# Attention and expert router on one core: sums of weights behind the centroids' products, codes behind the result's copy, first additions on GpSimd, logits and a drain earlier

## The chip, the cores and the metric

The kernel runs on one core of a Trainium2 chip. The core has TensorE (PE, matmuls; its weight loads are shown apart as PEld), VectorE (DVE), ScalarE (ACT), GpSimd (POOL) and SyncE (SP, which here issues most DMAs). Each engine works through its own queue in order. The metric is device time in microseconds (us) for one execution, less is better.

## The reference

The first half is attention inside clusters. Every query and every key of a head goes to the one of 16 centroids that it is nearest to, and a query attends only to keys of its own cluster. The second half sends every token (a row of all heads' results) to the one of 8 experts that it is nearest to, and multiplies that expert's result by the softmax weight of the choice.

```python
B, H, S, D = 4, 8, 768, 64          # 16 centroids per head
q_assign = argmax(q_n @ c_n.T); k_assign = argmax(k_n @ c_n.T)   # rows of unit length
scores = where(q_assign == k_assign, q @ k.T / sqrt(D), -1e9)
x = softmax(scores) @ v              # (B, H, S, D), then to (3072, 512)
logits = unit(x) @ unit(expert_emb).T / tau                      # 8 experts
e = argmax(logits); gate = softmax(logits)[e]
out = gate * (relu(x @ w1[e]) @ w2[e])       # w1 512x1024, w2 1024x512
```

All of it is in float32, apart from the cluster masks, which are exact in bfloat16.

## The kernel before

**Attention.** Two heads of one batch make a pair; there are 16 pairs, numbered n = 0 to 15, four for each batch b. A pair's work is cut into 12 units: two halves of the queries (groups 2n and 2n+1), and for each six blocks of 128 keys (j = 0 to 5). The main loop takes two units an iteration, so a pair has six iterations, it = 0 to 5. In an iteration the order is written out by hand: the scores of the next two units go to PE (`scores`, L484) and their exponentials to ACT (`expo`, L495); then `between(n, it)` puts in pieces of the next pair's preparation and of routing; then the two units of this iteration are multiplied with the values (`attend`, L506).

The exponentials are written to five rotating buffers, `probs`. A buffer is free for the exponential five units later when PE has read it in `attend` and when it has been added to `acc`, the running sum of the group's weights. The sum of the first two units (j = 1) is one instruction on DVE, L515, which also adds a tiny constant; the four that follow are plain additions, L525. Only two score buffers exist (`psS`), so the scores of a unit wait for the exponential of the unit two before.

**Behind a group.** After j = 5 ACT copies the group's result out of PSUM (`o_sb`, L530) and `unite` adds its two halves on GpSimd (L539; on DVE for the last pair). `total` sums `acc` over partitions on PE with a matrix of ones (L553) in a `misc` bank, of which there are two in turn; DVE transposes and inverts, and GpSimd spreads the inverses with eight small copies (L574). `divide` multiplies the result with the inverses (L585, L589), and `rows` transposes it and stores it to `x_rows` in HBM (L606, L613). `total` for a pair's two groups is called in the next pair's iteration 0 behind `attend`; `divide` in its iteration 2, `rows` in its iteration 3.

**Preparing a pair.** `prep_pieces` gives the steps: `turn0` and `turn1` transpose the queries and keys on DVE (L386), `products` multiplies them with the centroids on PE (L396) and transposes the outcome back on DVE (L405), `choose` finds the nearest centroid on DVE (L414 to L417), writes its code with three activations on ACT (`cd`, L419 and L422) and has SP transpose the codes by DMA into `hot` (L427). The scores of the next pair, which begin in iteration 5, read `hot`: a matmul of the codes adds the mask (L484, the bfloat16 ones).

```python
elif it == 0:
    piece(n + 1, "products")
elif it == 1:
    piece(n + 1, "choose")
elif it == 3:
    rows(2 * n - 2, 2 * n - 1)
```

The matmuls of scores and results use the array in four parts of 64x64; those of `products`, `total` and the router's logits use four parts of 128x32.

**Routing and experts.** A batch's router products (L632) and logits (`lt`, L644) are made in the next batch's pairs. For the last batch they come after the loop, in two halves: `route[b][0](0)`, the products of the first half, closes the loop; `logits(0)` and `products(1)` come later, among the first experts' blocks. From there PE works through the experts' blocks to the end: `hidden` L1261, `result` L1277, and for larger portions L1176 and L1213. GpSimd gathers tokens (L1041) and scatters results (L1052) with indirect DMAs. In the last attention pairs GpSimd also gathers the first experts' tokens (`fetch`, three in pair 14, iteration 3) and orders them (`order_x`, L1127).

Of the kernel before, what the change touches and what calls it, by code (L numbers as in the profile page):

```python
# [39 lines left out]
def kernel(  # L40
# [282 lines left out]
    def begin():  # L323

        nc.scalar.dma_start(out=c_sb, in_=centroids.rearrange("h c d -> (h c) d"))
        load(0, "q")
        load(0, "k")
        load(0, "v")
        load(1, "qk")
        constants()  # L330

        nc.scalar.activation(en_r, epsc[0:E], ACTF.Sqrt)
        nc.scalar.dma_start(out=emb, in_=moe_expert_emb)
        nc.scalar.dma_start(out=tau, in_=moe_tau.to_broadcast([E, 1]))
        norm_rows(cn_r, c_sb, P)
        unit_centroids()
        keep_up(2)
        piece(0, "turn0")
        piece(0, "turn1")
        norm_rows(en_r, emb, E)  # L340

        nc.scalar.activation(cn_r, epsc, ACTF.Exp)
        piece(0, "products")
        for m in range(2):
            scores(m, (1,))
        piece(0, "choose")
        keep_up(6)
        piece(0, "turn_numbers")
        for m in range(2):
            scores(m, (0,))  # L350
            expo(m)
        token_numbers()
        unit_experts()

    def prep_pieces(n):
# [51 lines left out]
        def choose():  # L407

            shp = [P, S // SQ, C]
            asn = t["asn"].rearrange("p (g c) -> p g c", c=C)  # L410
            amax = smp.tile(shp[0:2], F32, tag="amax", name="amax")
            sel = smp.tile(shp, BF16, tag="sel", name="sel", bufs=1)
            pm = smp.tile(shp[0:2], BF16, tag="pm", name="pm")
            nc.vector.tensor_reduce(amax, asn, axis=AXX, op=ALU.max)  # L414
            nc.vector.tensor_tensor(sel, asn, bc(amax, shp, 2), ALU.is_equal)
            nc.vector.tensor_tensor(sel, sel, bc(prefc, shp, 1), ALU.mult)
            nc.vector.tensor_reduce(pm, sel, axis=AXX, op=ALU.max)  # L417
            pm = pm.rearrange("p (s h) -> p s h", h=2)
            nc.scalar.activation(cd[..., 1], pm, ACTF.Copy, scale=wcd)  # L419
            for i, p0 in enumerate((0, D)):  # L420
                g = slice(p0, p0 + D)
                nc.scalar.activation(  # L422
                    cd[g, :, :, 2 * i], pm[g], ACTF.Square, scale=(BIG**0.5, 1.0)[i]
                )
            t["H"] = trp.tile([P, S // (2 * SQ), P], BF16, tag="hot", name="hot")
            if n > 0:
                nc.sync.dma_start_transpose(  # L427
                    out=t["H"], in_=cd.rearrange("p s h c -> p (s h c)")
                )

        def turn_numbers():
# [17 lines left out]
            "turn1": lambda: turn_blocks("k") if n else (turn("q", 1), turn("k", 1)),  # L449
            "products": products,  # L450
            "choose": choose,
            "turn_numbers": turn_numbers,
        }

# [42 lines left out]
    def attend(i):  # L497

        n, hq, j = units[i]
        d, g = un[i], gr[i // GU]  # L500
        if j == 0:
            g["o_ps"] = psO.tile([P, 2, 512], F32, tag="o_ps", name="o_ps")
        for h in range(2):
            for half in range(2):
                keys = slice(D * half, D * half + D)
                nc.tensor.matmul(  # L506
                    g["o_ps"][D * h : D * h + D, half, 0:HE],
                    lhsT=ld[n]["v"][keys, j, h],
                    rhs=d["prob"][keys, h, 0:HE],
                    start=(j == 0),  # L510
                    stop=(j == NJ - 1),
                )
        if j == 1:
            g["acc"] = xp.tile([P, 2, HS], F32, tag="acc", name="acc", bufs=3)
            nc.vector.scalar_tensor_tensor(  # L515
                out=g["acc"],
                in0=un[i - 1]["prob"][:, :, 0:HS],
                scalar=NJ * EPS,
                in1=d["prob"][:, :, 0:HS],
                op0=ALU.add,  # L520
                op1=ALU.add,
            )
            un[i - 1].clear()
        elif j > 1:
            nc.vector.tensor_tensor(g["acc"], g["acc"], d["prob"][:, :, 0:HS], ALU.add)  # L525
            d.clear()
        if j == NJ - 1:
            t = ld[n]
            t["o_sb"] = xp.tile([P, 2, HE], F32, tag="o_sb", name="o_sb", bufs=1)
            nc.scalar.copy(t["o_sb"], g["o_ps"][:, :, 0:HE])  # L530
# [801 lines left out]
    def between(n, it):  # L1332
        b, nb = divmod(n, NHP)
        if n == 0:

            if it == 0:
                piece(1, "turn0")
                piece(1, "turn1")
            elif it == 1:
                piece(1, "products")  # L1340
            elif it == 2:
                piece(1, "choose")
                turned_experts()
            elif it == 3:
                later_constants()
        elif it == 0:
            piece(n + 1, "products")
        elif it == 1:
            piece(n + 1, "choose")
        elif it == 3:  # L1350
            rows(2 * n - 2, 2 * n - 1)
        if it == 4:
            piece(n + 2, "turn0")
        elif it == 5:
            piece(n + 2, "turn1")
        if b > 0:
            if nb == 0 and it == 3:
                route[b - 1] = route_pieces(b - 1)
            products, logits, read, norms, choose = route.get(b - 1, (None,) * 5)


            m = NJ * nb + it
            if m in (8, 11, 14):
                read((m - 8) // 3 * 2, (m - 8) // 3 * 2 + 2)
            if m in (15, 16, 18, 19, 21, 22):
                norms((15, 16, 18, 19, 21, 22).index(m))
            if (nb, it) == (0, 4):
                products(0, 1)
            elif (nb, it) == (0, 5):
                logits(0, 1)  # L1370
            elif (nb, it) == (1, 4):
                choose()
# [29 lines left out]
    with tc.manual_schedule(engines=by_hand):  # L1402
        begin()
        for i in range(0, len(units), 2):
# [21 lines left out]
                turn_x(E0[0], nc.scalar.copy, xp.tile([P, DM], F32, tag="acc", name="xTm", bufs=3))  # L1426
            for m in range(i, i + 2):
                attend(m)
            if it == 2:
                if n > 0:  # L1430
                    divide(2 * n - 2, 2 * n - 1)
                unite(2 * n)
            elif it == 5:
                unite(2 * n + 1)
            if i + 2 == len(units):
                rows(ngroups - 2)
                route[b][0](0)
            if it == 0 and n > 0:
                total(2 * n - 2, 2 * n - 1)
            elif it == 3 and n == NP - 1:  # L1440
                total(2 * n)
        at.close()
        mop = ctx.enter_context(tc.tile_pool(name="mop", bufs=2, **tile_waits))
# [9 lines left out]
        pb = Places(1, rtb)  # L1453
        gates = gate_pieces(0, B - 1)
        gates[0]()
        hidden(E0[0], (0,))
        order_x(E0[3])
        total(ngroups - 1)
# [7 lines left out]
        hidden(E0[0], (1,))  # L1466
        gates[3]()
        weights1(E0[2])
        logits(0)
        read(0, NJ, P - SQ, P)  # L1470
        products(1)
        hidden(E0[1], (0,))
# [83 lines left out]
        for i, it in enumerate(later):  # L1556
# [9 lines left out]
                fetch(later[i + 2])  # L1566
            if i > 0 and later[i - 1].kind == "sized":
                send(later[i - 1])
            if it.kind == "sized":
                sized_hidden(it)  # L1570
            else:
# [66 lines left out]
```

## Time and profile before

| what | us |
|---|---|
| median of 3 timed runs | 716.82 (714.88 to 720.92) |
| the profiled execution's own time | 709.36 |
| its span, first to last instruction | 707.6 |
| PE busy in the span | 690.8 (98%) |
| attention loop, about | 16 to 334 |
| experts, about | 334 to 701 |

The profiled execution was faster than each of the three timed ones; times of steps come from it. "PE busy" contains modelled ends of matmuls, so it is read beside the times at which PE's matmuls start. A line of the timeline has its start in the span, its duration, the engine, the source line, what was done and how many instructions were merged; in square brackets stands how long the engine had been idle, and what ended that.

### The profile page before, as it was taken

How to read it: one execution, taken by the hardware profiler on the slowest of the kernel's cores; microseconds unless marked ns; L12 is line 12 of the kernel's file. 1: busy time of each engine (PE TensorE's matmuls, PEld its weight loads, DVE VectorE, ACT ScalarE, POOL GpSimd, SP SyncE). 2: the span in 40 equal slices, each digit the busy share in tenths (PEclk: the TensorE clock that was granted, in tenths of full speed). 3: DMA queues.
4: the chain of work that ended last, by engine and by line, in shares of the span. 5: the costliest groups of instructions: out<-in, count | busy, mean ns of one | idle time of the engine just before them, and what ended most of it. 6: DMA issues, size and time to landing. Idle time of an engine off the chain costs nothing.

```text
span 707.6 us, 16122 instructions
## 1 busy us (share of the span) xinstructions
PE 690.8 (98%) x6518; PEld 456.2 (64%) x6518; DVE 382.6 (54%) x665; ACT 265.1 (37%) x446; POOL 264.2 (37%) x402
## 2 busy tenths in 40 slices
PE   6999999999999999999899999999999999999995
PEld 3444444444444444455876668897979797979793
DVE  4788888989889999989483121340220303031210
ACT  4566665677566755676215110101010111111110
POOL 2122222322224222353213546736264554544412
PEclk9999999999999999999999999999999999999999
DMA  9536665886657678879798987268668686869450
GB/s 150 91 60 110 105 104 87 153 159 108 100 108 146 120 146 152 183 190 329 184 278 305 342 314 268 81 233 287 258 226 299 198 310 226 320 242 330 142 192 28
DMA packets 244124, 135.55 MB, mean 192 GB/s; under 512 B 207808, under 2 KB 207810, under 8 KB 244044
## 3 DMA queue, kind: packets, MB, share of 16 engines
q1 hardware_dynamic: 237852, 121.28, 64.0%
q0 software_dynamic: 6016, 13.12, 5.4%
q8 instruction: 54, 0.88, 0.5%
q14 instruction: 26, 0.21, 0.1%
q10 hardware_dynamic: 176, 0.05, 0.0%
HBM read 115.92 MB, written 13.12 MB: 182 GB/s over the span
## 4 chain that ended last, share of the span: by engine, by line
PE 79%; DVE 6%; DMA 5%; issue 5%; POOL 1%; SPq 1%; ACT 1%; POOLq 0%; DVEq 0%; ACTq 0%
PE s_ps L484 18%; PE o_ps L506 15%; PE y_ps L1277 10%; PE h_ps L1261 9%; PE h_ps L1176 9%; PE y_ps L1213 5%; PE misc L1213 5%; DMA out_dram<-ys,spidx 3%; PE x_ps L1176 3%; DVE acc L525 2%; DMA x_rows<-xb 2%; PE misc L396 2%; PE misc L553 2%; PE misc L632 1%; SPq L613 1%
## 5 line engine op out<-in xcount | busy, mean ns | idle before, releaser
L495 ACT ACTIVATE prob<-s_ps 128x768 f32<-128x768 f32 x192 | 153.7, 812 | 95.2 <-PE s_ps L484 82.1
L484 PE MATMUL s_ps<-qT,kT 64*64 64x384 f32 x1536 | 156.0, 482 | 0.0
L506 PE MATMUL o_ps<-prob,v 64*64 64x385 f32 x1536 | 142.0, 486 | 0.0
L525 DVE TENSOR_TENSOR acc<-acc,prob 128x768 f32<-128x768 f32 x128 | 125.6, 982 | 8.8 <-ACT cd L422 0.5
L506 PEld LDWEIGHTS o_ps<-prob,v 64*64 64x64 f32 x1536 | 54.6, 133 | 70.3 <-issue 58.5
L1261 PE MATMUL h_ps<-xTm,w1s 128*128 128x128 f32 x768 | 90.0, 278 | 0.0
L1261 PEld LDWEIGHTS h_ps<-xTm,w1s 128*128 128x128 f32 x768 | 89.0, 195 | 1.4 <-issue 1.0
L1222 DVE STREAM_TRANSPOSE ys<-y_ps 128x256 f32<-128x256 f32 (+4 forms) x16 | 6.7, 417 | 153.4 <-PE y_ps L1213 153.4
L539 POOL TENSOR_TENSOR o_sum<-o_sb 128x385 f32<-128x385 f32 x30 | 32.0, 1067 | 146.3 <-ACT o_sb L530 146.3
L1052 POOL DMA_INDIRECT out_dram<-ys,spidx x56 | 56.7, 1013 | 74.7 <-DVE ys L1236 59.8
L1277 PE MATMUL y_ps<-w2s,hT 128*128 128x512 f32 x192 | 84.5, 593 | 0.0
L484 PEld LDWEIGHTS s_ps<-qT,kT 64*64 64x64 f32 x1536 | 56.0, 133 | 38.1 <-issue 34.9
L1176 PE MATMUL h_ps<-xTs,w1s 128*128 128x272 f32 (+7 forms) x384 | 72.9, 346 | 1.1 <-ACTq L1537 1.1
L1176 PEld LDWEIGHTS h_ps<-xTs,w1s 128*128 128x128 f32 x384 | 66.6, 190 | 8.0 <-issue 2.4
L1268 ACT ACTIVATE hT<-h_ps 128x512 f32<-128x512 f32 x24 | 14.3, 596 | 148.1 <-PE h_ps L1261 148.1
L484 PE MATMUL s_ps<-hot 64*64 64x384 bf16 x768 | 64.7, 325 | 2.2 <-ACT prob L495 1.1
L1041 POOL DMA_INDIRECT xs<-x_rows,gpidx x56 | 57.3, 1023 | 17.1 <-issue 16.8
L574 POOL COPY inv<-inv 32x12 f32<-32x12 f32 x120 | 43.0, 358 | 54.6 <-DVE inv L571 50.2
L1277 PEld LDWEIGHTS y_ps<-w2s,hT 128*128 128x128 f32 x192 | 35.6, 190 | 40.2 <-issue 40.2
L484 PEld LDWEIGHTS <-hot 64*64 64x64 bf16 x768 | 23.6, 106 | 39.4 <-issue 38.1
L1213 PE MATMUL y_ps<-hTs,w2o 128*128 128x272 f32 (+7 forms) x256 | 48.0, 346 | 0.0
L1213 PE MATMUL misc<-hTs,w2o 128*128 128x272 f32 (+7 forms) x256 | 48.0, 346 | 0.0
(264 smaller groups left out, 679.5 us busy)
## 6 DMA issues: line engine op xcount, KB each, us to landing
w1s<-in_moe_w_dram SPq DMA_DIRECT2D x18, 2048.0 KB, 10.6
w2s<-in_moe_w_dram SPq DMA_DIRECT2D x18, 2048.0 KB, 13.3
v<-in_v_dram SPq DMA_DIRECT2D x128, 48.0 KB, 2.1
q<-in_q_dram SPq DMA_DIRECT2D x60, 96.0 KB, 3.4
k<-in_k_dram SPq DMA_DIRECT2D x60, 96.0 KB, 3.6
x_rows<-xb SPq DMA_DIRECT2D x60, 96.0 KB, 2.8
xr<-x_rows SPq DMA_DIRECT2D x9, 512.0 KB, 4.0
w1s<-in_moe_w_dram SPq DMA_DIRECT2D x4, 1024.0 KB, 9.9
```

Source lines behind the costliest of these rows:

```text
L484: nc.tensor.matmul(s_ps[D * half : D * half + D, h, 0:HS], lhsT=l[rows, half], rhs=r[rows], start=part == (1 if len(parts) < 2 else 0), st ...
L495: nc.scalar.activation(d["prob"][:, :, 0:HS], d["s_ps"][:, :, 0:HS], ACTF.Exp, scale=scale)
L506: nc.tensor.matmul(g["o_ps"][D * h : D * h + D, half, 0:HE], lhsT=ld[n]["v"][keys, j, h], rhs=d["prob"][keys, h, 0:HE], start=(j == 0), st ...
L525: nc.vector.tensor_tensor(g["acc"], g["acc"], d["prob"][:, :, 0:HS], ALU.add)
L539: add(t["o_sum"][:, hq], t["o_sb"][:, 0], t["o_sb"][:, 1], ALU.add)
L574: nc.gpsimd.tensor_copy(inv2[M * to : M * to + M, :, i % 2], inv[M * i : M * i + M])
L1041: nc.gpsimd.indirect_dma_start(out=to, out_offset=None, in_=of, in_offset=bass.IndirectOffsetOnAxis(ap=at, axis=0), bounds_check=n - 1, oo ...
L1052: inst = nc.gpsimd.indirect_dma_start(out=to, out_offset=bass.IndirectOffsetOnAxis(ap=at, axis=0), in_=of, in_offset=None, bounds_check=n - 1,
L1176: nc.tensor.matmul(bk, lhsT=w1s[it.slot][:, c, P * f : P * f + P], rhs=d["xT"][:, c, 0:C], start=(c == 0), stop=(c == KD - 1),)
L1213: nc.tensor.matmul(bks[g][:, 0:C], lhsT=d["w2"][:, f, P * g : P * g + P], rhs=d["hT"][:, f, 0:C], start=(f == 0), stop=(f == KF - 1),)
L1261: nc.tensor.matmul(bk[:, m : m + P], lhsT=w1s[it.slot][:, c, f0 + m : f0 + m + P], rhs=d["xT"][:, P * c : P * c + P], start=(c == 0), stop ...
L1277: nc.tensor.matmul(bk, lhsT=d["hT"][:, P * c : P * c + P], rhs=w2s[it.slot][:, c], start=(c == 0), stop=(c == KF - 1),)
```

## The change

- `choose` is cut in two: the activations on ACT and the DMA of the codes become a piece of their own, `codes`, called in iteration 2 after `attend`, behind the result's copy of that iteration.
- In a pair's loop `turn0` of pair n+2 moves from iteration 4 to 5, `turn1` of the next pair from iteration 5 to the following iteration 0, `products` from 0 to 1, `choose` from 1 to 2, `rows` from 3 to 4. `total` moves from iteration 0 behind `attend` to iteration 1, directly behind `products`. `divide` moves from 2 to 3, `unite` of the first group from 2 to 3 and of the second from iteration 5 to the next pair's iteration 0. The earlier batches' router products move from iteration 4 to 5, their logits from 5 to the next pair's iteration 0.
- The first addition of each group (j = 1) goes to GpSimd as a plain addition, and the tiny constant is added at j = 2 on DVE, in the form that L515 had.
- For the last batch `logits(0)` moves ahead of the first expert's `hidden`.
- GpSimd gets a `drain` behind the last large scatter, ahead of the last block's scatter.

```diff
         piece(0, "choose")
+        piece(0, "codes")
...
-            pm = pm.rearrange("p (s h) -> p s h", h=2)
+            t["pm"] = pm.rearrange("p (s h) -> p s h", h=2)
+
+        def codes():
+            pm = t["pm"]
             nc.scalar.activation(cd[..., 1], pm, ACTF.Copy, scale=wcd)
...
         if j == 1:
             g["acc"] = xp.tile([P, 2, HS], F32, tag="acc", name="acc", bufs=3)
+            nc.gpsimd.tensor_tensor(
+                g["acc"], un[i - 1]["prob"][:, :, 0:HS], d["prob"][:, :, 0:HS], ALU.add
+            )
+            un[i - 1].clear()
+        elif j == 2:
             nc.vector.scalar_tensor_tensor(
                 out=g["acc"],
-                in0=un[i - 1]["prob"][:, :, 0:HS],
+                in0=g["acc"],
                 scalar=NJ * EPS,
                 in1=d["prob"][:, :, 0:HS],
                 op0=ALU.add,
                 op1=ALU.add,
             )
-            un[i - 1].clear()
+            d.clear()
...
         elif it == 0:
+            piece(n + 1, "turn1")
+        elif it == 1:
             piece(n + 1, "products")
-        elif it == 1:
+            total(2 * n - 2, 2 * n - 1)
+        elif it == 2:
             piece(n + 1, "choose")
-        elif it == 3:
+        elif it == 4:
             rows(2 * n - 2, 2 * n - 1)
-        if it == 4:
+        if it == 5:
             piece(n + 2, "turn0")
-        elif it == 5:
-            piece(n + 2, "turn1")
...
-            if (nb, it) == (0, 4):
+            if (nb, it) == (0, 5):
                 products(0, 1)
-            elif (nb, it) == (0, 5):
+            elif (nb, it) == (1, 0):
                 logits(0, 1)
...
+            if it == 0 and n > 0:
+                unite(2 * n - 1)
             if it == 2:
-                if n > 0:
-                    divide(2 * n - 2, 2 * n - 1)
+                piece(n + 1, "codes")
+            if it == 3 and n > 0:
+                divide(2 * n - 2, 2 * n - 1)
+            if it == (3 if n + 1 < NP else 2):
                 unite(2 * n)
-            elif it == 5:
+            elif it == 5 and n + 1 == NP:
                 unite(2 * n + 1)
...
-            if it == 0 and n > 0:
-                total(2 * n - 2, 2 * n - 1)
-            elif it == 3 and n == NP - 1:
+            if it == 3 and n == NP - 1:
                 total(2 * n)
...
         gates[0]()
+        logits(0)
         hidden(E0[0], (0,))
...
-        logits(0)
         read(0, NJ, P - SQ, P)
         products(1)
...
                 send(later[i - 1])
+                if i == LAST:
+                    nc.gpsimd.drain()
```

More of the change, by code (lines that the diff above doesn't have):

```diff
@@ L451, in prep_pieces @@
             "choose": choose,
+            "codes": codes,
             "turn_numbers": turn_numbers,
```

## The prediction

> **What bounds the kernel now.** I read the page's busy times first, then the same by stages, then PE's waits, then the timeline of one pair.
>
> ```profile
> PE 690.8 (98%) x6518; PEld 456.2 (64%) x6518; DVE 382.6 (54%) x665; ACT 265.1 (37%) x446; POOL 264.2 (37%) x402
> ...
> 193.96:213.29 19.33, 19.33 (x268) 8.80 (x264) 15.96 (x26) 11.86 (x17) 6.12 (x12) 1.00 0.56 112
> ...
> 253.27:275.22 21.95, 21.75 (x301) 10.05 (x297) 21.08 (x31) 12.53 (x18) 6.02 (x11) 1.00 0.80 149
> ...
> PE s_ps L484 <- ACT prob L495: 1.1, 2, 0.7
> ...
> PE misc L632 <- DVE lt L644: 2.1, 1, 2.1
> ```
>
> PE is never idle for long. The rows by stage are pair 9 and pair 12 (length; then busy time of PE, PEld, DVE, ACT, POOL; clock; DMA share and GB/s): in pair 9 DVE works 15.96 of 19.33 us, in pair 12 21.08 of 21.95, so there DVE is about as late as PE. Only two waits of PE matter to this change: 1.1 us for exponentials, and 2.1 us for DVE's logits behind the loop. What can be won lies in what PE does between its matmuls, in pairs 11 and 12, behind the loop, and at the end.
>
> **Sums behind products.** The timeline, PE alone, first pair 9, iterations 0 and 1, then pair 4 with the router's products:
>
> ```profile
> 193.96 0.34 PE L484 MATMUL s_ps<-hot 64*64 64x384 bf16 x4
> ...
> 195.68 0.52 PE L396 MATMUL misc<-qT,cnB 128*32 128x384 f32 x2
> ...
> 196.47 1.52 PE L506 MATMUL o_ps<-prob,v 64*64 64x385 f32 x16
> ...
> 197.92 0.88 PE L553 MATMUL misc<-acc,ones 128*32 128x192 f32 x16
> 198.73 0.36 PE L484 MATMUL s_ps<-hot 64*64 64x384 bf16 x4
> ...
> 107.65 0.33 PE L484 MATMUL s_ps<-hot 64*64 64x384 bf16 x4
> ...
> 109.37 1.51 PE L632 MATMUL misc<-xT,embT 128*32 128x192 f32 x32
> ...
> 112.15 0.34 PE L484 MATMUL s_ps<-hot 64*64 64x384 bf16 x4
> ```
>
> A plain iteration takes 2.91 (201.66 to 204.57). Iteration 0 of pair 9 takes 198.73 - 193.96 = 4.77: products and sums, apart, cost 1.86. The router's products move the same columns in the same shape (32 x 192 = 6144; products 8 x 384 and sums 16 x 192 also 6144), in one block, and cost 112.15 - 107.65 - 2.91 = 1.59. So one block instead of two saves 0.27, in the 14 pairs that have both (1 to 14): **-3.8**. From below nothing, if the sums' DVE data came late; they are ready an iteration earlier. The new place costs nothing else on PE.
>
> **First additions on GpSimd.** DVE loses 32 instructions L515 at 0.94 (30.2 us), but L525 at j = 2 becomes the L515 form, which costs the same. So DVE is relieved by 2 x 0.92 = 1.84 a pair. GpSimd has no row for 128x768. Its nearest row, L539, takes 0.86 alone for 128x385, so I take 1.73; with DVE beside it that row reached 1.67, twice as much, so up to 3.4. GpSimd was busy 6.12 of 19.33 and gets 3.5 to 7 more. The two engines disturb each other:
>
> ```profile
> 214.39 2.61 DVE L525 TENSOR_TENSOR acc<-acc,prob 128x768 f32<-128x768 f32 x2
> 215.33 0.85 POOL L539 TENSOR_TENSOR o_sum<-o_sb 128x385 f32<-128x385 f32 x1
> ```
>
> Two additions that took 2.01 at 211.56 took 2.61 here beside 0.85 of GpSimd: 0.7 us lost per us of overlap. The addition of iteration 0 starts when DVE has little but a one-input transpose; the one of iteration 3 lies beside `choose`. I take 1.2 us of DVE lost a pair (2 x 1.73 x 0.7, half of it overlapped), from 0 to 3.5 (DVE stopped for both additions, 2 x 1.73). Net relief is 0.6, from 1.84 to a loss of 1.6.
>
> The Trainium skill (SBUF — State Buffer, section "SBUF: two separate sides") speaks against the change: DVE with two SBUF inputs and GpSimd share a port pair as an exclusive lock, held for a whole instruction, so that the other engine stands still. The row agrees that the loser waits, though 0.6 and not 0.85. By the rule alone the relief would turn into the loss at the end of that range, and the sum into the second rival's.
>
> The walk of the queue: the exponential that needs the buffer freed by iteration 3's addition is the second of iteration 4, some 4.5 us after iteration 3 starts. GpSimd's inverses (3.08 for eight) are done about when iteration 3 starts, so the addition has 4.5 us for 1.73 to 3.4. It is hidden. In pair 14 it is not: three gathers stand ahead of it on GpSimd (1.25, 0.99 and 1.00, with 0.3 between them: 3.9). Their indices were written at 305.4; `choose` (1.96) now stands ahead of them on DVE in the same iteration, so about 307.4, and 307.4 + 3.9 + 1.73 = 313.0; the exponential behind it began at 311.31 before and feeds a matmul due at 312.32. PE waits **+1.5** (0.5 to 3).
>
> What the relief buys: in pair 11 iteration 0 took 5.29 and iteration 2 3.40, in pair 12 iteration 0 took 5.79; over 4.77, 2.91 and 4.77 that is 0.52 + 0.49 + 1.02 = 2.03 lost by a late DVE. I take half, **-1.0** (0 to -2.0).
>
> **Codes behind the copy.** ACT and SP in pair 9, iterations 2 and 3:
>
> ```profile
> 201.76 0.40 ACT L419 ACTIVATE cd<-pm,wcd 128x24 bf16<-128x24 bf16 x1 [0.34 <-DVE pm L417]
> ...
> 201.98 0.61 ACT L422 ACTIVATE cd<-pm 64x24 bf16<-64x24 bf16 x2
> ...
> 202.62 1.65 SPq L427 DMA_TRANSPOSE hot<-cd  x1
> ...
> 204.87 0.80 ACT L530 COPY o_sb<-o_ps 128x770 f32<-128x770 f32 x1 [0.54 <-PE o_ps L506]
> ...
> 205.62 1.62 ACT L495 ACTIVATE prob<-s_ps 128x768 f32<-128x768 f32 x2
> ...
> 210.38 0.33 PE L484 MATMUL s_ps<-hot 64*64 64x384 bf16 x4
> ```
>
> Codes take 0.83 (201.76 to 202.59). Behind the copy they run 205.67 to 206.50, and the two exponentials end at 207.31 and 208.12. Their score buffers are due at 207.48 and 208.28: 0.16 to spare, so nothing lost. `choose` (1.96) ends about 0.4 before the codes want it, if DVE isn't behind. The DMA starts near 206.55; `hot` is read at 210.38, which leaves 3.7. Landings were 3.2 to 4.9, median 3.3: nothing lost at the median. On SP the eight `v` loads (3.91) and, in some pairs, a read of `x_rows` (0.44) now stand ahead of it, free to go before the codes are ready; the query loads, the first expert's weights and `rows` stand behind it, all with iterations to spare. Cost **0** (up to 1.2 a pair at 4.9).
>
> **Logits earlier.** PE's 2.08 before L632 (342.55 to 344.63) was for `lt`, 0.24 long at the end of a DVE queue. Moved ahead, it can run from 333.9. Next to be late is the second half's result, ready at 341.65; with 0.24 more ahead of it 341.9, before 342.55. `divide` and `rows` of the last pairs, an iteration later, can eat 0.6 more. **-2.0** (-1.0 to -2.1). PE has one wait behind that place (1.1, on a branch, which stays), so the gain lasts.
>
> **Drain.** The last lines on GpSimd and SP:
>
> ```profile
> L1633 POOLq DRAIN  x3: 40/113/6017, 700.7 to 707.3; - x3
> L1633 SPq DRAIN  x3: 7/7/13, 704.2 to 707.0; - x3
> ```
>
> GpSimd's drain begins at 700.7 and takes 6.02, to 706.72; SP, which waits for all landings, is through at 704.3. So the drain alone holds the end for 2.4. Drains with little behind them took 0.04 to 0.19, which suggests that its length follows what has gathered since the last one; an earlier drain would then take most of it away. It falls into GpSimd's pause before the last scatter (7.41), longer than the longest drain. **-1.6** (0 to -2.4).
>
> **Sum.** -3.8 + 1.5 - 1.0 + 0 - 2.0 - 1.6 = -6.9, on the profiled execution's 709.36 (span 707.6, 1.76 around it): 702.5. That execution was 7.5 below the median of the timed runs; I take the difference over, 716.82 - 6.9 = **709.9**. No measurement of this kernel tells less than about 1%, 7.2 us, from no change.
>
> **Rivals.**
>
> *All hidden costs stay hidden* (0.15): the drain's full 2.4, the whole backlog of 2.03 and only 0.5 in pair 14: -3.8 + 0.5 - 2.0 - 2.0 - 2.4 = -9.7, 707.1. For it speaks that DVE has 3.4 us free in pair 9; against it that pairs 11 and 12 have almost none.
>
> *GpSimd's additions hold DVE* (0.12): with 3.5 lost for 1.84 relieved, pairs 10 to 14 get 1.6 more DVE work each, and in 11 and 12 DVE is already as late as PE. Three such pairs lose 5 where the backlog was to give 1.0: -6.9 + 6 = -0.9, 715.9. For it speaks the row above, against it that the quiet pairs keep 15.96 - 1.84 + 3.5 = 17.6 of 19.05. It decides once the loss passes 1.84 a pair.
>
> *The codes' DMA lands late* (0.10, the slower case): one mechanism, PE waiting for `hot` in iteration 5. For it: 4.9 was seen, in pair 14, and the slack shrinks to 0.4 over the median; against it: 3.24 and 3.28 in pairs 5 and 13, with eight loads behind. At 4.9 each of 15 pairs loses 1.2, +18 - 6.9 = +11, 728. Slower than before from a landing of 4.2.
>
> *The drain does nothing* belongs to the forecast's range: -5.3, 711.5.
>
> **How the numbers follow.** My forecast has 0.63, with -5 to -9 inside its terms' bounds, 708 to 712, and the timed runs spread by 6 us. A little under half of it is faster by over 1%, the rest within 1%: 0.28 and 0.35. The first rival adds 0.15 to faster; the second 0.07 to the same and 0.05 to slower; the third 0.10 to slower. Faster 0.43, same 0.42, slower 0.15. The range 705 to 717.5 leaves out the third rival and the far ends.
>
> **What would show it.** After, PE has L396 and L553 side by side and iteration 1 takes 4.5, iteration 0 2.91; a quiet pair 19.05 for 19.33. PE's wait for `lt` is gone. Iterations 3 and 4 stay at 2.91; longer ones mean exponentials or `hot` were late, and PE's waits would name L495 or L427. L525 rows of 1.5 and more beside GpSimd's additions measure the lock. GpSimd's last drain ends near SP's. I am wrong if GpSimd's additions take over 4.5, or if the last drain still takes 6.

## The result and the profile after

The changed kernel took **726.79 us** (median of 6 runs, 725.37 to 728.32), the kernel before 716.14 beside it (6 runs, 713.96 to 720.92). The ratio is 1.0152, with a 95% interval of 1.0132 to 1.0171: slower by 1.5%, where 1% faster was forecast. In a second comparison it took 725.79 against 712.60, ratio 1.0176 (1.0150 to 1.0203). The profiled execution took 728.32, its span is 726.4.

From the page of the changed kernel: busy times, and the groups of the two kinds of additions (line, engine, operation, shapes, count; busy us and mean ns of one).

```profile
PE 699.9 (96%) x6518; PEld 477.5 (66%) x6518; DVE 399.2 (55%) x633; ACT 263.0 (36%) x446; POOL 341.2 (47%) x434
...
L535 DVE TENSOR_TENSOR acc<-acc,prob 128x768 f32<-128x768 f32 x96 | 136.5, 1422 | 7.0
...
L520 POOL TENSOR_TENSOR acc<-prob,prob 128x768 f32<-128x768 f32 x32 | 59.8, 1868 | 79.2 <-ACT prob L500 78.1
```

DVE has 32 instructions fewer (633 for 665) and is busy 16.6 us longer. Its plain additions, L535 (L525 before), average 1.42 us; before, 128 of them averaged 0.98. GpSimd's additions take 1.87, near the 1.73 that was estimated.

The stages that answer to those shown of before, pair 9 and pair 12 (length; busy PE, PEld, DVE, ACT, POOL; clock; DMA):

```profile
202.81:222.22 19.41, 19.25 (x268) 9.94 (x264) 17.15 (x25) 11.12 (x16) 8.48 (x13) 1.00 0.60 119
...
266.29:290.28 23.99, 22.21 (x301) 11.73 (x297) 22.64 (x29) 12.37 (x18) 11.74 (x14) 1.00 0.74 145
```

Pair 9 is 0.08 longer than the 19.33 of before, pair 12 2.04 longer than 21.95. PE, which had no idle time to speak of in the loop, now has some. The waits of PE and of ACT in the changed kernel (us in total, times, longest):

```profile
PE s_ps L489 <- ACT prob L500: 6.0, 11, 1.6
PE misc L397 <- DVE kT L387: 1.8, 3, 0.7
PE s_ps L489 <- DMA hot<-cd: 1.7, 2, 1.1
```

```profile
ACT prob L500 <- DVE acc L535: 32.9, 41, 2.7
ACT prob L500 <- DVE acc L525: 9.4, 11, 1.8
```

The waits for additions in the kernel before (L515 is the first addition of a group, L525 the plain ones):

```profile
ACT prob L495 <- DVE acc L515: 7.1, 14, 1.1
ACT prob L495 <- DVE acc L525: 4.7, 9, 1.6
```

Together 11.8 us before and 42.3 now: the exponentials wait for buffers that DVE should have released. PE's wait for `lt` (2.1 before) is gone; a wait of 0.5 for `xT` stands behind the loop instead.

The length of each iteration, from the starts of PE's scores, says where the time lies (us, for pairs 1 to 9, then for 10 to 14):

| iteration | before | after |
|---|---|---|
| 0 | 4.76 to 4.77; 5.07, 5.29, 5.79, 4.77, 4.76 | 2.91; 4.97, 3.70, 4.07, 2.91, 3.59 |
| 1 | 2.93 throughout | 4.54 to 6.03; 4.83, 6.68, 6.39, 4.86, 6.12 |
| 4, plain | 2.91 | 3.2, but 4.02 and 3.92 in pairs 5 and 6, 4.20 in 14 |
| 5, plain | 2.91 | 2.91 to 2.93, but 3.53 in pair 14 |

From iteration 0 of pair 1 to iteration 4 of pair 15, called **the loop** from here on, it is 291.7 before and 309.5 after: +17.8. All behind that, **the tail**, is 379.7 before and 379.1 after in the first profile and 376.3 in the second profile of the same kernel. Iteration 0 of pair 0 is 4.17 in some profiles and 5.4 to 5.8 in others, also where nothing was changed ahead of it (5.80 in the experiment with logits and drain alone), so it is not counted for or against the change. In every profile where it is long, the granted clock is 0.50 for 3.41 us from about 17; in the others it is not.

### The profile page after: what moved, and what is told of

Same layout as the page of the kernel before. It is cut to its first block, busy times and chain, and to the rows that moved or that the text cites. A ratio compares the mean times of both kernels' runs of the same rounds, so it can differ in the third digit from the quotient of the medians.

```text
span 726.4 us, 16166 instructions
## 1 busy us (share of the span) xinstructions
PE 699.9 (96%) x6518; PEld 477.5 (66%) x6518; DVE 399.2 (55%) x633; ACT 263.0 (36%) x446; POOL 341.2 (47%) x434
## 4 chain that ended last, share of the span: by engine, by line
PE 62%; DVE 19%; issue 8%; DMA 5%; ACT 2%; POOL 2%; SPq 1%; POOLq 0%; DVEq 0%; ACTq 0%
PE h_ps L1271 10%; PE y_ps L1287 10%; PE s_ps L489 9%; PE h_ps L1186 9%; DVE acc L535 7%; PE o_ps L511 6%; PE misc L1223 5%; PE y_ps L1223 5%; DMA out_dram<-ys,spidx 3%; PE x_ps L1186 3%; DVE acc L525 2%; PE misc L397 2%; PE misc L563 2%; ACT prob L500 2%; DVE xT L599 1%
## 5 line engine op out<-in xcount | busy, mean ns | idle before, releaser
L500 ACT ACTIVATE prob<-s_ps 128x768 f32<-128x768 f32 x192 | 152.0, 810 | 120.3 <-PE s_ps L489 75.0
L489 PE MATMUL s_ps<-qT,kT 64*64 64x384 f32 x1536 | 160.4, 486 | 0.0
L511 PE MATMUL o_ps<-prob,v 64*64 64x385 f32 x1536 | 144.2, 486 | 0.0
L535 DVE TENSOR_TENSOR acc<-acc,prob 128x768 f32<-128x768 f32 x96 | 136.5, 1422 | 7.0
L511 PEld LDWEIGHTS o_ps<-prob,v 64*64 64x64 f32 x1536 | 62.5, 133 | 59.5 <-issue 53.2
L520 POOL TENSOR_TENSOR acc<-prob,prob 128x768 f32<-128x768 f32 x32 | 59.8, 1868 | 79.2 <-ACT prob L500 78.1
L489 PEld LDWEIGHTS s_ps<-qT,kT 64*64 64x64 f32 x1536 | 62.4, 134 | 28.5 <-issue 26.6
L584 POOL COPY inv<-inv 32x12 f32<-32x12 f32 x120 | 49.9, 416 | 64.0 <-DVE inv L581 59.6
L489 PE MATMUL s_ps<-hot 64*64 64x384 bf16 x768 | 69.1, 327 | 10.4 <-ACT prob L500 6.0
L489 PEld LDWEIGHTS <-hot 64*64 64x64 bf16 x768 | 30.7, 106 | 55.3 <-issue 49.1
```

Of the source, the lines that this page charges most:

```text
L489: nc.tensor.matmul(s_ps[D * half : D * half + D, h, 0:HS], lhsT=l[rows, half], rhs=r[rows], start=part == (1 if len(parts) < 2 else 0), st ...
L500: nc.scalar.activation(d["prob"][:, :, 0:HS], d["s_ps"][:, :, 0:HS], ACTF.Exp, scale=scale)
L511: nc.tensor.matmul(g["o_ps"][D * h : D * h + D, half, 0:HE], lhsT=ld[n]["v"][keys, j, h], rhs=d["prob"][keys, h, 0:HE], start=(j == 0), st ...
L520: nc.gpsimd.tensor_tensor(g["acc"], un[i - 1]["prob"][:, :, 0:HS], d["prob"][:, :, 0:HS], ALU.add)
L584: nc.gpsimd.tensor_copy(inv2[M * to : M * to + M, :, i % 2], inv[M * i : M * i + M])
```

## Experiments

Times are medians beside runs of the kernel before on the same chip. The chips differ: in the four groups of runs, on three chips, the kernel before took 709.6, 712.6, 712.9 and 712.3. So ratios are compared, and for stages the lengths in the traces.

| kernel | us | before, same chip | ratio (95%) |
|---|---|---|---|
| changed kernel again | 725.79 | 712.60 | 1.0176 (1.0150 to 1.0203) |
| before + additions on GpSimd | 716.68 | 709.60 | 1.0100 (1.0071 to 1.0130) |
| changed, additions on DVE | 708.80 | 709.60 | 0.9988 (0.9977 to 0.9999) |
| before + logits + drain | 703.32 | 709.60 | 0.9908 (0.9889 to 0.9928) |
| changed, `unite` early | 716.12 | 712.60 | 1.0047 (1.0031 to 1.0064) |
| changed, additions on DVE, codes at `choose` | 715.43 | 712.60 | 1.0036 (1.0020 to 1.0051) |
| before + merged block + logits + drain | 703.42 | 712.60 | 0.9868 (0.9842 to 0.9894) |
| before + drain | 710.37 | 712.92 | 0.9965 (0.9953 to 0.9978) |
| before + merged block | 710.75 | 712.92 | 0.9968 (0.9954 to 0.9982) |
| changed, additions on DVE, turns early | 716.12 | 712.30 | 1.0049 (1.0031 to 1.0067) |

### The additions, alone and taken back

Before with the additions on GpSimd alone:

```diff
         if j == 1:
-            nc.vector.scalar_tensor_tensor(out=g["acc"], in0=..., scalar=NJ * EPS, ...)
+            nc.gpsimd.tensor_tensor(g["acc"], ..., d["prob"][:, :, 0:HS], ALU.add)
+        elif j == 2:
+            nc.vector.scalar_tensor_tensor(out=g["acc"], in0=g["acc"], scalar=NJ * EPS, ...)
```

> The kernel before with one part of the change alone: each group's first addition (j = 1) on GpSimd, the tiny constant added at j = 2. Theory 1 (GpSimd's additions hold VectorE, its additions beside them take 1.7 to 2.6 us for 0.96, and exponentials and the next pair's keys come late for it): additions L525 (the plain ones) average 1.2 us and more, TensorE waits for exponentials, and the time rises by 6 to 15 us, ratio 1.008 to 1.021. Theory 2 (the delay comes from the codes that now stand ahead of the exponentials on ScalarE) and theory 3 (the shifted order itself makes VectorE's work collide): time within 2 us of the kernel before, or 1 to 2 us less since VectorE has 32 instructions fewer.

The changed kernel with the reverse of this edit:

> The changed kernel with the first additions back on VectorE; all other parts stay (order, merged sums, codes behind the copy, logits, drain). Theory 1 (GpSimd's additions hold VectorE): the plain additions are back at 0.96 to 1.0, iteration 1 is 4.55 in all pairs up to 9, and the time is 5 to 9 us below the kernel before, ratio 0.987 to 0.993. Theory 2 (codes ahead of the exponentials): iteration 4 stays at 3.2 for 2.91 in each pair, 0.3 x 14 = 4.2 us, and the landing of the codes still costs about 1.7 us; ratio 0.995 to 1.000. Theory 3 (the shifted order): most of the 18 us lost in the loop stay, ratio above 1.005.

Alone the additions cost 7.1 us, with a loop of 299.6. Without them the changed kernel is at 0.9988, and its loop falls from 309.5 to 296.3: they are worth **13.2 us** there. Iteration by iteration, with the changed kernel's second profile, 8.2 of these lie in iteration 1 (0.8 each in pairs 2, 3, 4 and 8), 3.1 in iteration 4 (0.3 in most pairs), 1.1 in iteration 0 and 0.8 in iteration 5 of pair 14. Iteration 4 of the quiet pairs is back at 2.91, so theory 2's 0.3 there came from the additions, not from the codes. Theory 1 holds for the larger part, though 0.9988 is above its 0.987 to 0.993 (and in theory 2's range, for another reason): something else in the change takes back what merged sums, logits and drain give. Theory 1's number for the additions alone did not hold: the plain additions average 1.01 there, not 1.2 and more. So GpSimd's additions don't hold DVE's additions everywhere. The timeline of the changed kernel, pair 2, iteration 3 (start, duration; DVE, GpSimd and one of ACT):

```profile
68.88 1.82 POOL L520 TENSOR_TENSOR acc<-prob,prob 128x768 f32<-128x768 f32 x1
...
69.01 2.50 DVE L535 TENSOR_TENSOR acc<-acc,prob 128x768 f32<-128x768 f32 x1
...
70.65 1.58 POOL L549 TENSOR_TENSOR o_sum<-o_sb 128x385 f32<-128x385 f32 x1
...
71.60 0.81 ACT L500 ACTIVATE prob<-s_ps 128x768 f32<-128x768 f32 x1 [0.34 <-DVE acc L535]
71.61 1.43 DVE L535 TENSOR_TENSOR acc<-acc,prob 128x768 f32<-128x768 f32 x1
```

The two engines take turns, one instruction at a time. GpSimd's addition ends at 70.70; DVE's, begun at 69.01, ends 0.81 later, at 71.51. Then `o_sum`, recorded from 70.65, ends at 72.23, 0.72 behind that; then DVE's next ends at 73.04, again 0.81 behind. The two DVE additions are those of the group that just ended, and the exponentials of iteration 4 want the buffers they release.

The same place with the additions alone in the order of before, pair 2, iteration 3:

```profile
67.54 0.97 DVE L590 STREAM_TRANSPOSE den<-inv 128x768 f32<-128x768 f32 x1
68.55 2.45 DVE L594 SCALAR_TENSOR_TENSOR xT<-o_sum,den 128x768 f32<-128x768 f32 x1
```

```profile
67.54 0.86 POOL L544 TENSOR_TENSOR o_sum<-o_sb 128x385 f32<-128x385 f32 x1 [2.86 <-ACT o_sb L535]
68.36 1.82 POOL L515 TENSOR_TENSOR acc<-prob,prob 128x768 f32<-128x768 f32 x1
```

Here `o_sum` stands ahead of the addition in GpSimd's queue and waits for ACT's copy, so the addition begins 2.02 into the iteration instead of 0.42. DVE's last additions are over by then. What is held is `divide` (2.45 for 1.02), for which nobody waits soon. In a quiet pair this costs nothing: iterations 1 and 4 stay at 2.93 and 2.91. Most of the loss of this kernel lies in pair 11 (iteration 0, 7.48 for 5.28) and pair 14 (iteration 5, 7.07 for 2.91). In pair 14 the addition comes late in GpSimd's own queue: it began 0.69 into iteration 5, behind the three gathers; up to 1.7 of the 4.16 lost come on top (half of 3.41), from 3.41 us at a granted clock of 0.50 that begin with the end of that wait. In pair 11 two small router steps on DVE are held:

```profile
235.76 0.86 POOL L544 TENSOR_TENSOR o_sum<-o_sb 128x385 f32<-128x385 f32 x1 [6.48 <-ACT o_sb L535]
235.96 0.70 DVE L869 TENSOR_TENSOR whicha<-io_f,ranka 1x32 f32<-1x32 f32 x1
...
236.58 1.83 POOL L515 TENSOR_TENSOR acc<-prob,prob 128x768 f32<-128x768 f32 x1
236.70 1.76 DVE L752 TENSOR_TENSOR picka<-whicha,io_f 1x32 f32<-1x32 f32 x1
```

They took 0.14 and 0.74 before. The last two additions of the group stand behind them on DVE and begin 4.62 into the iteration, for 2.43 before.

### The place of `unite`

```diff
-            if it == 0 and n > 0:
-                unite(2 * n - 1)
...
-            if it == (3 if n + 1 < NP else 2):
+            if it == 2:
                 unite(2 * n)
-            elif it == 5 and n + 1 == NP:
+            elif it == 5:
                 unite(2 * n + 1)
```

> The changed kernel with the calls of unite (the sum of a result's two halves on GpSimd) back at the end of iterations 2 and 5, ahead of GpSimd's first additions in its queue; all else stays. Theory 1a (what costs is where GpSimd's additions stand: in the changed kernel each starts 0.4 us into iteration 0 or 3, beside the last two additions of the group before, which free buffers that exponentials wait for; with o_sum ahead, which waits for ScalarE's copy, they start some 2.1 us in, as in the kernel that has only this part): the plain additions average 1.0 to 1.1 instead of 1.42, ScalarE's waits for additions fall from 42 to under 15 us, and 6 to 11 of the 13 us come back: ratio 0.998 to 1.006. Theory 1b (GpSimd's additions cost as such, wherever they stand): ratio above 1.009.

1.0047, and a loop of 300.1: 9.4 of the 13.2 us are back, with GpSimd's additions kept. Plain additions average 1.07. Pair 2, iteration 3, GpSimd, and then ACT's waits:

```profile
68.78 1.10 POOL L549 TENSOR_TENSOR o_sum<-o_sb 128x385 f32<-128x385 f32 x1 [0.79 <-ACT o_sb L540]
69.84 2.53 POOL L520 TENSOR_TENSOR acc<-prob,prob 128x768 f32<-128x768 f32 x1
```

```profile
ACT prob L500 <- POOL acc L520: 7.6, 5, 4.5
ACT prob L500 <- DVE acc L535: 7.2, 6, 3.4
```

Iteration 3 begins at 67.59, so the addition starts 2.25 in. ACT's wait for the plain additions fell from 32.9 to 7.2. What is left is 7.6 of waiting for GpSimd itself: iteration 1 of pair 11 is 8.80 (5.79 with the additions on DVE), iteration 5 of pair 14 6.59 (2.93). Iteration 1 of pair 11 also holds 3.41 us at a granted clock of 0.50, which makes up to 1.7 of it. So theory 1a holds: most of the cost is where GpSimd's additions stand, and most of the rest is GpSimd's queue in two pairs.

### What GpSimd reads

```diff
-            nc.gpsimd.tensor_tensor(
-                g["acc"], un[i - 1]["prob"][:, :, 0:HS], d["prob"][:, :, 0:HS], ALU.add
-            )
+            nc.gpsimd.tensor_copy(g["acc"], d["prob"][:, :, 0:HS])
```

> The changed kernel with GpSimd's first addition replaced by a copy of the second of the two blocks (the first block of each group's weights is left out of the sum). GpSimd then reads one operand instead of two. If what stops VectorE's additions is that GpSimd holds the way to SBUF for the length of its instruction, whatever it reads, an addition that begins during the copy ends about 0.9 us behind the copy's end, as now (2.5 us for an addition that begins 0.14 us into a GpSimd addition of 1.82), and its length follows that of the copy. If it is the two operands' traffic, the additions beside the copy take under 1.3 us. The profile decides, not the time.

The sums lack a block, so the tokens fall to other experts, and of its 768.6 us only the loop is read (294.9). Pair 1, iteration 3:

```profile
48.32 0.82 POOL L520 COPY acc<-prob 128x768 f32<-128x768 f32 x1
...
48.48 1.48 DVE L533 TENSOR_TENSOR acc<-acc,prob 128x768 f32<-128x768 f32 x1
...
49.11 1.57 POOL L547 TENSOR_TENSOR o_sum<-o_sb 128x385 f32<-128x385 f32 x1
```

The copy ends at 49.14 and the addition at 49.96, 0.82 behind it: the copy with one operand stops DVE's addition as wholly as the addition with two. Its harm is less because it is half as long. DVE's instructions with one input are not stopped: the transpose L387 at 57.63 in the changed kernel takes 0.97 wholly beside a GpSimd addition.

### Codes behind the copy

```diff
             piece(n + 1, "choose")
+            piece(n + 1, "codes")
...
-            if it == 2:
-                piece(n + 1, "codes")
```

(the changed kernel, additions on DVE)

> The changed kernel with the additions on VectorE and the codes' activations and DMA back behind choose, ahead of iteration 2's exponentials; order, merged sums, logits and drain as in the changed kernel. Theory 2 (codes behind the copy make hot land late in some pairs): iteration 4 of pairs 5, 6 and 14 goes from 4.0, 4.1 and 4.2 back to 2.91, TensorE's wait for hot (3.1 us) is gone, the time falls from 708.8 to about 705.3, ratio 0.992 to 0.995. Rival (the landing is late for the shift of choose by an iteration, or the codes ahead of the exponentials delay those by as much): no difference from the kernel with the codes behind the copy, ratio 0.997 to 1.000.

Iterations 4 of pairs 5, 6 and 14 went from 4.03, 4.09 and 4.24 to 2.91, 2.91 and 3.37, and PE's waits for `hot` are gone. But iteration 3 rose from 2.91 to 3.77 in 12 of the pairs 1 to 14 (4.08 in 11, 3.22 in 14), and the ratio from 0.9988 to 1.0036: neither number was met. PE's waits of this kernel name why:

```profile
PE o_ps L511 <- ACT o_sb L535: 8.6, 13, 0.9
```

With `choose` an iteration later, its result comes from DVE some 0.7 into iteration 3. Activations that wait for it ahead of the copy stop ACT's queue, the copy is late, and the result's bank with it. So the codes behind the copy save what the shifted `choose` would cost, and pay for it with a late transfer in three pairs. That the codes' place alone makes `hot` late is not shown. With the codes at `choose` the transfer is issued 1.57 into iteration 3 instead of 1.99, and 5.11 are left for it instead of 3.83; but 0.86 of the 1.28 more is the longer iteration 3. Before, with `choose` an iteration earlier, it was issued 0.96 into iteration 2, with 7.8 left: most of the slack went with the shift of `choose`. The waits and the transfer's row in the kernel with the codes behind the copy and the additions on DVE:

```profile
PE s_ps L489 <- DMA hot<-cd: 3.1, 3, 1.1
```

```profile
hot<-cd SPq DMA_TRANSPOSE x1, 5.0
```

That is pair 6: issued 1.99 into iteration 3, landed 4.96 later, where 0.92 + 2.91 = 3.83 were left.

### Turns early

```diff
-        elif it == 0:
-            piece(n + 1, "turn1")
...
-        if it == 5:
+        if it == 4:
             piece(n + 2, "turn0")
+        elif it == 5:
+            piece(n + 2, "turn1")
```

(the changed kernel, additions on DVE)

> The changed kernel with the additions on VectorE and with turn0 and turn1 (VectorE's transposes of the next pairs' queries and keys) back in iterations 4 and 5 instead of 5 and 0; all else shifted as in the changed kernel. Without the turns back, pairs 10, 11, 12 and 14 lose 4.4 us, and in pair 11 the keys' transpose ends at 240.8, 1.25 after the products of iteration 1 could start. Theory 3a (the late turns hold the products in pairs with a full VectorE): iterations 0 and 1 of pairs 10, 11, 12 and 14 (9.4, 9.1, 9.5 and 8.4 us) lose 0.5 to 1.2 each, the time falls by 2 to 4 us against the kernel without this edit, ratio 0.993 to 0.996. Theory 3b (a full VectorE is late with whatever stands in these iterations): the same 4.4 us reappear as waits for additions, ratio 0.997 to 1.000.

Both theories are missed: 1.0049, a loop of 302.3 for 296.3 (up to 1.7 of the 5.9 come from 3.41 us at a granted clock of 0.50 in pair 10). The transposes now stand ahead of the group's last additions on DVE, beside `rows`, whose transpose had been moved to that place. ACT's wait in this kernel, and in the one without the edit:

```profile
ACT prob L500 <- DVE acc L530: 28.3, 28, 2.7
```

```profile
ACT prob L500 <- DVE acc L530: 7.8, 9, 1.8
```

It supports 3b's mechanism (DVE is late with what stands ahead of its additions), at more than 3b's price. It doesn't settle which of the shifted pieces makes pairs 10, 11, 12 and 14 longer. The kernel of the experiment before this one says something on it: with the codes at `choose` and all else shifted, iterations 0 and 1 of these pairs take 8.1, 7.7, 7.8 and 7.4 us (a quiet pair 7.45), so most of their loss is gone there, and so is PE's wait for `cumx` in pair 10. Iteration 3 is 0.86 longer in most pairs of that kernel, which gives DVE time. So the shift doesn't by itself make DVE late; whether the codes' place or that time does it was not separated.

### Logits, drain, and the merged block

```diff
         gates[0]()
+        logits(0)
         hidden(E0[0], (0,))
...
                 send(later[i - 1])
+                if i == LAST:
+                    nc.gpsimd.drain()
```

> The kernel before with the last two parts alone: the last batch's first logits ahead of the first expert's block, and GpSimd's drain ahead of the last scatter. In the changed kernel's profile the wait for the logits fell from 2.08 to 0.51 us and the end after the last scatter came 2.1 us sooner, yet the time from iteration 4 of pair 15 to the end fell by 0.6 only, because TensorE paused 4.8 us at five places between. If those pauses are chance or the chip's, this kernel is 3.5 to 5.5 us faster than the kernel before, ratio 0.992 to 0.995. If the earlier logits or the drain bring the pauses with them, 0 to 1 us, ratio 0.998 to 1.000.

> The kernel before with the drain alone. The profile of logits and drain together has the span's end 4.23 us behind the last scatter's start, 6.63 without. If the drain alone does that, 2.4 us, ratio 0.9955 to 0.9975, and TensorE's wait for lt with the slow block behind it (granted clock 0.51) stays. If the drain only moves the wait: 0.999 to 1.001.

Together 0.9908, the drain alone 0.9965: 6.3 and 2.5 us, so some 3.7 are the logits' (the two were measured on different chips). The first is more than either theory had. The drain's rows in the changed kernel (shortest/median/longest ns, first and last start):

```profile
L1648 POOLq DRAIN  x3: 46/113/2945, 721.6 to 726.1; - x3
L1648 SPq DRAIN  x3: 7/7/13, 725.5 to 725.8; - x3
```

The last drain takes 2.95 for 6.02 and ends at 724.6, ahead of SP's at 725.5; the landings set the end now. From the last scatter's start to the end of the span it is 4.55 in the changed kernel, 4.23 with logits and drain or the drain alone, and 6.63 before.

What made the logits worth more than their wait is in the kernel before, PE around that wait, with the granted clock (the seventh number after the stretch's bounds, here 0.69 and 0.51):

```profile
344.70 0.87 PE L632 MATMUL misc<-xT,embT 128*32 128x96 f32 x32 [2.08 <-DVE lt L644]
345.50 5.47 PE L1261 MATMUL h_ps<-xTm,w1s 128*128 128x128 f32 x32
```

```profile
345.50:347.50 2.00, 2.00 (x16) 2.00 (x13) 1.41 (x7) 0.00 (x0) 0.24 (x2) 0.69 0.06 12
347.50:349.70 2.20, 2.20 (x13) 2.20 (x12) 0.00 (x0) 0.00 (x0) 1.24 (x6) 0.51 0.73 140
```

And the same block with the logits early:

```profile
344.28 0.87 PE L632 MATMUL misc<-xT,embT 128*32 128x96 f32 x32
345.07 3.84 PE L1261 MATMUL h_ps<-xTm,w1s 128*128 128x128 f32 x32
```

The block behind the wait takes 5.47 for 3.84: some 3.4 us at half the clock, which begin about 1.6 us after the wait is over. Without the wait there is no slow stretch there: 2.08 + 1.63 = 3.7.

The merged block without any shift:

```diff
-        elif it == 0:
-            piece(n + 1, "products")
...
             if it == 0 and n > 0:
+                piece(n + 1, "products")
                 total(2 * n - 2, 2 * n - 1)
```

> The kernel before with the products of iteration 0 called behind attend, directly ahead of total, and nothing else. The prediction's term: 0.27 a pair in 14 pairs, 3.8 us. From the profile with logits and drain: 0.28 a quiet pair, 0.4 lost in pair 10 and 0.5 in pair 14: 2 us, ratio 0.996 to 0.9985.

> The kernel before with the logits and the drain as in the changed kernel, and with the next pair's products called behind the results of iteration 0, directly ahead of total, so that products and sums make one block without moving anything else. Theory 3 (merging is worth 0.25 a pair, and the shift of the rest by an iteration is what made VectorE late in pairs 10 to 12 and 14): iteration 0 of a quiet pair 4.53 for 4.77, pairs 10 to 14 no longer than before, 3.3 us less than with logits and drain alone, 700.0 us, ratio 0.985 to 0.988. Rival (products later, so choose and the codes later, make the pairs with a busy VectorE longer): 0.990 or more.

Alone 0.9968, with logits and drain **0.9868 (703.4 us), the lowest ratio of all**, and faster than both kernels. PE in pair 1, iteration 0, of the merged block alone:

```profile
39.17 1.47 PE L506 MATMUL o_ps<-prob,v 64*64 64x385 f32 x16
40.57 0.52 PE L396 MATMUL misc<-qT,cnB 128*32 128x384 f32 x2
...
41.24 0.87 PE L553 MATMUL misc<-acc,ones 128*32 128x192 f32 x16
42.04 0.36 PE L484 MATMUL s_ps<-hot 64*64 64x384 bf16 x4
```

Iteration 0 takes 4.49 for 4.77, 0.28 a quiet pair, and iterations 1 to 5 stay at 2.91 to 2.93. Pairs 11 and 12 stay as they were (5.27, 5.78), pair 10 loses (5.46 for 5.07). So theory 3 has its half: merging needs no shift. Its other half, that the shift makes DVE late, is not shown by itself; it rests on the loops: 292.2 to 289.3 for the merged block alone, 291.8 to 296.3 for merged block, shift and codes behind the copy.

### The kernels again

> The kernel before, unchanged, run again beside the others so that their profiles have a reference from the same chip. Every theory: the times of the kernel before, 714 to 721 us, ratio 1.000. Its profile shows whether the rest behind the loop (379.7 us from iteration 4 of pair 15 to the end in the first profile) and the one-off pauses of TensorE in the experts' blocks differ from one execution to the next; the first profile had none of the pauses named 'issue' (nothing that the profile shows), the changed kernel's had 2.9 us of them.

> The kernel before, unchanged, for a profile on this chip. Its timed runs stood at 709.6 us on one chip and at 712.6 and 716 on two others, and the one profile shown first at 709.36. If this chip is one of the slower ones, the profile shows where the 3 to 7 us lie: TensorE paused about 1.2 us in the hidden block some 75 us behind iteration 4 of pair 15 in every kernel profiled on the second chip, and never on the first. Every theory: ratio 1.000.

> The changed kernel, unchanged, beside the others on the same chip. All theories of the loop: 720 us against 709.6 before, ratio 1.013 to 1.017, of it 13 us between this kernel and the one with the additions back on VectorE. The pauses of TensorE behind 400 us that are named 'issue' or had no counterpart before (4.8 us in five places in the first profile): if they come from the kernel, they are here again and the time from iteration 4 of pair 15 to the end is 379; if they are chance, it is 374, as in the kernel with the additions on VectorE (373.8).

The kernel before has a span of 707.6 on the first of these chips, as in the profile shown first, and 709.9 on another. There its tail is 381.3 for 379.7, with a pause of 0.7 in a hidden block some 75 us behind iteration 4 of pair 15, which the first chip does not show. The changed kernel's tail was 379.1 and then 376.3, so neither guess of the expectation (379 or 374) was met. In the three kernels with the additions on DVE it was 373.8 on one chip, 375.7 and 376.0 on two others. So most of these pauses come and go with the chip and the execution, and are not the change's.

## Why the prediction was wrong

| step | forecast | measured | from |
|---|---|---|---|
| sums behind products | -3.8 | -3.4 | 19.33 to 19.09 in a quiet pair without GpSimd's additions, 14 pairs |
| additions on GpSimd, pair 14, backlog | +0.5 | +13.2 | loops, 309.5 and 296.3 |
| the shifted order in pairs 10, 11, 12, 14 | none | +4.4 | their lengths, less the merged block and `hot` |
| codes behind the copy | 0 | +3.6 | iteration 4 of pairs 5, 6 and 14; 3.1 of it named as waits for `hot` |
| logits | -2.0 | -3.7 | trace: 2.08 and 1.63; medians 3.7 |
| drain | -1.6 | -2.4 | 6.63 to 4.23; median 2.5; 2.1 in the changed kernel's profile |
| sum | -6.9 | +11.7 | runs: +10.65 and +13.2 in the two comparisons |

**The step that failed is "First additions on GpSimd".** It said: "The addition of iteration 0 starts when DVE has little but a one-input transpose; the one of iteration 3 lies beside `choose`." Its walk of the queue then asked only whether GpSimd's own addition is in time ("It is hidden"), not which DVE instruction it stops. In the changed order the addition starts 0.4 into its iteration, because `unite` no longer stands ahead of it, and lies beside the last two additions of the group before. The loss of DVE was taken as 1.2 us a pair, from 0 to 3.5. The 96 plain additions, 0.44 longer each, make 42 us, 2.6 a pair, inside these bounds. But the price was then worked out as DVE's time: a quiet pair had 3.4 us free, so it could pay. What counted was which instruction was late: the two that release the exponentials' buffers ended 1.2 to 1.5 us later than with the additions on DVE (pair 2, iterations 0 and 3), and PE paid 0.3 to 1.5 in iterations 1 and 4 of most quiet pairs. A share of busy time can't show that. The +1.5 that was put at pair 14 for a late GpSimd addition is 0.6 there (iteration 5, 3.53 for 2.93).

**The row behind it was read as a rate.** Two additions with 0.85 of GpSimd beside them took 2.61 for 2.01, read as 0.7 us lost per us of overlap. It was one addition stopped whole: GpSimd's instruction ran from 215.33 to 216.18, and the second addition ended at 217.00, 0.82 after it. The Trainium skill (SBUF — State Buffer, section "SBUF: two separate sides") says that whichever starts first gets the pair for the whole instruction and the other fully blocks, for DVE instructions with two SBUF inputs against GpSimd ones that read SBUF. The timeline of pair 2 agrees to 0.1 us, for both directions, and the run with the copy for one operand too. The prediction set the row against the rule, where the row was an instance of it.

**The rivals.** "GpSimd's additions hold DVE" named the mechanism and priced it at +6, in pairs 10 to 14 only; 7.2 of the 13.2 lie in pairs 1 to 9. "The codes' DMA lands late" had the right price for one landing (1.2 at 4.9; iteration 4 grew by 1.1 to 1.3, and pair 6's landing took 4.96) and happened in 3 pairs of 15. The forecast's 0 took the median landing for all of them.

**Sums behind products** was right in kind and nearly in size, 0.24 to 0.28 a pair for 0.27. That "the new place costs nothing else on PE" failed: behind the shift, pairs 10, 11, 12 and 14 lost 4.4 us where the backlog was to give 1.0 back. In pair 10 PE waits 0.9 for GpSimd's `cumx`, which the products had covered. The rest is DVE being late; which of the moved pieces makes it so is open: putting the turns back made it worse, and with the codes at `choose` most of it was gone.

**Logits** were undersized since the stretch at half the clock behind the wait was not priced; the granted clock was there in the profile of before. **Drain** reached its bound of 2.4. "Drains follow what has gathered since the last one" agrees with the last drain's 2.95 for 6.02 behind an early one of 8.9.

What the forecast asked the profile to show: products and sums side by side and a quiet iteration 1 of 4.5 came true (pairs 1, 5 and 9); PE's wait for `lt` went; iteration 4 did not stay at 2.91; additions of 1.5 and more measured the lock. Neither of its two signs of being wrong came (GpSimd's additions took at most 2.54, the last drain 2.95): they watched GpSimd, and the failure lay in DVE's additions.

## What to carry to other kernels

Before an operation goes to another engine, look at what lies beside it in the new order and who waits for that, not at the free share of the engine it leaves: an instruction that releases a buffer is worth more than its length. A measured slow-down beside another engine is first read as "who waits for whose end", with starts and ends, and only then as a rate. When a piece is moved in one queue, what stood ahead of it in another may go: here a call moved on GpSimd decided when an addition began, and 9 us hung on it.

## What the runs showed of the hardware

- In the changed kernel a GpSimd addition of 128x768 or 128x385 and a DVE addition with two inputs in SBUF never ran at once. In all 48 cases where DVE's addition was issued during GpSimd's, it ended 0.81 to 0.82 after GpSimd's end (alone it takes about 0.9). `o_sum`, issued during DVE's addition, ended 0.72 to 0.73 after DVE's end (alone 0.86), and a one-operand copy on GpSimd stopped DVE's addition too.
- A wait of PE of 2.08 us cost 1.63 more, as matmuls that had started every 0.11 then started every 0.21 for about 3.4 us at a granted clock of 0.51. The same wait (2.08 or 2.09) stands in six profiles, and in each such a stretch begins 0.03 to 1.6 after it. The Trainium skill (TensorE: Matmul & The Clock Gate, Part 1) tells of half rate behind an idle window of about 3.4 us and of as much busy time to leave it. The length of the slow stretch agrees; the way into it does not, since here pauses of 2.08 were followed by one. The length of a pause alone doesn't decide it: in the loop, pauses of 2.29 (`unite` early) and 2.41 (additions alone) were followed by such a stretch, those of 2.00 (additions alone) and 3.51 (`unite` early) were not, and with the turns early one began behind waits of 1.0. What else decides is open.
- GpSimd's drain behind the last scatters took 6.02 without an earlier one, and 2.95 behind an earlier one of 8.9, which ended in the pause ahead of the last scatter.
